# Attention scores of units 10 to 35 from float16 halves that transfers make

## The chip, the cores and the metric

One core of a Trainium2 chip runs the whole program in one launch. The metric is the device time of one execution in microseconds, the median of several runs. The engines are TensorE (PE; its weight loads are shown as PEld), VectorE (DVE), ScalarE (ACT), GpSimd (POOL) and SyncE (SP), and 16 DMA engines move data.

## The reference, cut to what matters

Attention within chunks of 64 positions, then two feed-forward stages, of which only the first lines bear on the change:

```python
scores = scale * np.matmul(q_c, k_c.transpose(0, 1, 2, 4, 3))     # 64x64 per chunk and head
scores = scores - np.max(scores, axis=-1, keepdims=True)
attn = np.exp(scores)
attn = attn / (np.sum(attn, axis=-1, keepdims=True) + 1e-09)
out = np.matmul(attn, v_c)
...
xn = (x - mu) / np.sqrt(var + 1e-06) * g_ln
ch = np.maximum(xn @ w_ch1, 0.0) @ w_ch2
return (x + ch).astype(np.float32)
```

There are 8 batches, 8 heads and 576 positions (9 chunks of 64), model width 512 and a feed-forward width of 2048. A third stage (`_moe2_ref`) follows and is not touched.

## The kernel before

**Units and blocks.** The 72 chunks of all batches are taken two at a time: 36 units, numbered 0 to 35, of 128 rows x 512. Two units make a block; 18 blocks go through the first feed-forward stage. `attention(t)` (L301) does one unit, `norm` (L439) its layer norm, and a DMA transpose (`transpose`, L265) puts the normalised rows, as two float16 halves, into the tile `xT` of the block. The products of the first feed-forward layer (`ff1p`, L737, its matmul at L750) read `xT`; those of the second (`ff2p`, L786, matmul at L802) read its results from `arena`. From block 3 on, one step of a block is 24 matmuls of L750 and 21 of L802, and a block has eight steps.

**Halves.** A float32 operand is split into a float16 `hi` and the float16 remainder `lo`, and a product is done as hi*hi + hi*lo + lo*hi, three float16 matmuls.

**A unit.** `scores(t)` (L279) loads q and k of the unit by one transfer on SP (L283) into a float32 tile, `qk` or, from unit 10 (`JOIN`) on, the single buffer `qkl`, and does 16 float32 matmuls of 64x64 (L291). VectorE takes maxima (L389) and subtracts them (L390), ScalarE takes the exponentials (L393). Up to unit 13 (`BYDMA` is 14) the probabilities are turned by four float32 matmuls against the identity (L337), copied from PSUM by ScalarE (`pt`, L416), and multiplied with v by 16 float32 matmuls (L361). From unit 14 on, ScalarE and VectorE split them into halves (`ph`, L400 and L401), a DMA transpose on SP turns these (`ptt`, L404), v is split as well (`vq`, L408 and L409), and 48 float16 matmuls of 64x64 do the product (L349). VectorE then divides (L430), takes the statistics (L462, L463), POOL the inverse root (L457, L460), VectorE normalises (L466), ScalarE and POOL make the two halves `hl` (L469, L471), and SP issues the transpose into `xT` (L474).

**Joint steps.** From unit 10 on the values product of a unit and the scores of the next are one item of TensorE's queue (L429):

```python
scores(t + 1, o)
a_, qk_ = started[t + 1]
o("PE", 1260, lambda: (pv_(), qk_()), rd=pp() + [a_], wr=[kp, ks])
```

**What sets the order.** Everything is recorded first (`Plan.op`) with an engine, an assumed duration, a priority and an assumed delay to its users on other engines (`lat`). `Plan.run` then deals the items out greedily, each engine taking the item of lowest priority number among those that its model holds ready, and so fixes the order of each engine's queue. Each engine runs its queue strictly in that order. A unit t has priority 10t and goes ahead of the feed-forward products, at 1000 and above, as soon as the model holds its inputs ready.

Of the kernel before, what the change touches and what calls it, by code (L numbers as in the profile page):

```python
# [9 lines left out]
F16 = mybir.dt.float16  # L10
F32 = mybir.dt.float32
# [3 lines left out]
AF = mybir.ActivationFunctionType  # L15
ALU = mybir.AluOpType
# [8 lines left out]
    a=[2264, -1991, -1698, -26, -1734, 4025, 2562, -374],  # L25
# [15 lines left out]
    f=[-277, -1680, 2543],  # L41
# [106 lines left out]
def fused_kernel(ctx: ExitStack, tc, qkv, w1, w2, g1, w_in, w_out, wsgt, wsgs, g2, b_sg, out):  # L148
# [122 lines left out]
    def palloc(tag, bufs, shape, dt, pool=None):  # L271
        return plan.buf(tag, bufs, lambda: (pool or pools["att"][1]).tile(shape, dt, tag=tag, name=tag, bufs=bufs))
# [1 line left out]
    x_t = {}  # L274
    xT_t = {}
    started = {}
    BYDMA = 14

    def scores(t, o):  # L279

        a = palloc("qk", 2, [P, 2, 512], F32) if t < JOIN else palloc("qkl", 1, [P, 2, 512], F32)
        src = qkv[t].rearrange("p (a f) -> p a f", a=3)
        o("SP", 1700, lambda: nc.sync.dma_start(out=a.t, in_=src[:, 0:2]), wr=[a], lat=2200 if t < JOIN else 4000)  # L283
        s2 = pair[t % 2 if t < 6 else 1]

        def qk():
            for hp in range(4):
                for r in (slice(0, 64), slice(64, 128)):
                    for c in range(2):
                        k = hp * 128 + c * 64  # L290
                        nc.tensor.matmul(  # L291
                            s2[64 * c:64 * c + 64, r.start // 64, hp * 64:hp * 64 + 64],
                            lhsT=a.t[r, 0, k:k + 64],
                            rhs=a.t[r, 1, k:k + 64],
                            start=True,
                            stop=True,
                        )

        started[t] = a, qk

    def attention(t):  # L301
        n = t % 2 if t < 6 else 1
# [7 lines left out]
        def o(eng, ns, fn, **k):  # L310
            ns = FAST.get((eng, ns), ns)
            op(eng, ns, fn, prio=k.pop("prio", pr), lat=k.pop("lat", lat), **k)

        if t not in started:
            scores(t, o)
            a, qk = started[t]
            o("PE", 1260 * z, qk, rd=[a], wr=[ks])
        v = palloc("v", 2, [P, 512], F32) if t < JOIN else palloc("vl", 1, [P, 512], F32)
        o("SP", 730, lambda: nc.sync.dma_start(out=v.t, in_=qkv[t].rearrange("p (a f) -> p a f", a=3)[:, 2]), wr=[v], lat=2200)
        mx = palloc("mx", 2, [P, 2, 4, 1], F32)  # L320
        pm = palloc("pm", 2, [P, 4, 2, 64], F32) if t < JOIN else palloc("pml", 1, [P, 4, 2, 64], F32)
        sm = palloc("sm", 2, [P, 4, 2, 1], F32)
        rd = palloc("rd", 2, [P, 4, 2, 1], F32)
        pt = palloc("pt", 1, [P, 4, 128], F32) if t < BYDMA else None
        if t in (4, 5):
            x = plan.buf(f"x{t}", 1, lambda: pools["att"][1].tile([P, 512], F32, name=f"x{t}", bufs=1))
        else:
# [13 lines left out]
        def pv_():  # L341
            if t >= BYDMA:
                for hp in range(4):
                    for n, (y, z) in enumerate(((0, 0), (0, 1), (1, 0))):
                        for r in (slice(0, 64), slice(64, 128)):
                            for c in range(2):
                                k = c * 256 + hp * 64
                                q = hp * 128 + c * 64
                                nc.tensor.matmul(  # L349
                                    s2[64 * c:64 * c + 64, r.start // 64, 256 + hp * 64:256 + hp * 64 + 64],  # L350
                                    lhsT=ptt[0].t[r, y, q:q + 64],
                                    rhs=vq[0].t[r, z, k:k + 64],
                                    start=(n == 0),
                                    stop=(n == 2),
                                )
                return
            for hp in range(4):
                for r in (slice(0, 64), slice(64, 128)):
                    for c in range(2):
                        k = c * 256 + hp * 64  # L360
                        nc.tensor.matmul(  # L361
                            s2[64 * c:64 * c + 64, r.start // 64, 256 + hp * 64:256 + hp * 64 + 64],
                            lhsT=pt.t[r, hp, 64 * c:64 * c + 64],
                            rhs=v.t[r, k:k + 64],
                            start=True,
                            stop=True,
                        )
# [56 lines left out]
        if t < JOIN or t + 1 == NT:  # L424
            o("PE", 1260 * z, pv_, rd=pp(), wr=[kp])
        else:
            scores(t + 1, o)
            a_, qk_ = started[t + 1]
            o("PE", 1260, lambda: (pv_(), qk_()), rd=pp() + [a_], wr=[kp, ks])  # L429
        o("DVE", 600, lambda: nc.vector.tensor_tensor(  # L430
            out=x.t.rearrange("p (h a d) -> p a h d", h=4, a=2),
            in0=pv,
# [6 lines left out]
    def norm(t, x, o):  # L439

        bs = palloc("bs", 2, [P, 6], F32)
        mv = palloc("mv", 2, [P, 2], F32)
        rs = palloc("rs", 2, [P, 1], F32)
        xn = palloc("xn", 1, [P, 512], F32)
        hl = palloc("hl", 2, [P, 2, 512], F16)
        b = t // 2
        c0 = (t % 2 if b < B0 else 1 - t % 2) * 128
        if t % 2 == 0:
            if b == 2:
                xT_t[b] = plan.buf("xT2", 1, lambda: stage.tile([P, 2, 4, 256], F16, name="xT2"))  # L450
            else:
                xT_t[b] = palloc("xT", 2, [P, 2, 4, 256], F16, px)
        xT = xT_t[b]
        x_t[t] = x

        def rs_():
            nc.gpsimd.tensor_scalar(  # L457
                out=rs.t, in0=mv.t[:, 1:2], scalar1=1.0, scalar2=1e-6, op0=ALU.mult, op1=ALU.add
            )
            nc.gpsimd.tensor_tensor(out=rs.t, in0=rs.t, in1=cpow, op=ALU.pow)  # L460

        o("DVE", 600, lambda: nc.vector.bn_stats(out=bs.t, in_=x.t), rd=[x], wr=[bs])  # L462
        o("DVE", 70, lambda: nc.vector.bn_aggr(out=mv.t, in_=bs.t), rd=[bs], wr=[mv])  # L463
        o("POOL", 730, rs_, rd=[mv, "cpow"], wr=[rs], two=2)
        xe = ("POOL", 830, nc.gpsimd) if t < 8 and TUNE['xn'][t] else ("DVE", 460, nc.vector)
        o(xe[0], xe[1], lambda: xe[2].tensor_scalar(  # L466
            out=xn.t, in0=x.t, scalar1=mv.t[:, 0:1], scalar2=rs.t, op0=ALU.subtract, op1=ALU.mult
        ), rd=[x, mv, rs], wr=[xn], two=1 + (xe[0] == "POOL"))
        o("ACT", 520, lambda: nc.scalar.activation(out=hl.t[:, 0], in_=xn.t, func=AF.Copy), rd=[xn], wr=[hl])  # L469
        lo = ("DVE", 600, nc.vector) if t < 8 and TUNE['lo'][t] else ("POOL", 1110, nc.gpsimd)  # L470
        o(lo[0], lo[1], lambda: lo[2].tensor_tensor(  # L471
            out=hl.t[:, 1], in0=xn.t, in1=hl.t[:, 0], op=ALU.subtract
        ), rd=[xn], wr=[hl], two=1)
        o("SP", 1100, lambda: transpose(xT.t, slice(c0, c0 + 128), hl.t), rd=[hl], wr=[xT], lat=2200)  # L474
# [379 lines left out]

    bW = {"top": Buf("topB", None)}

    ATT = [f"{n}{k}" for n in ("qk", "v", "mx", "pm", "sm", "rd", "bs", "mv", "rs", "hl") for k in range(2)] + ["pt", "xn", "qkl", "vl", "u0", "u1", "pml", "ph", "ptt", "vq"]
    w2s = {}

    def open_sums():  # L860
# [822 lines left out]
```

## Time and profile before

| | |
|---|---|
| median of 3 runs | 1177.54 us (1176.41 to 1178.52) |
| the profiled execution | 1177.76 us, of which the span of its trace is 1175.7 us |
| TensorE matmul busy | 1163.7 us, 99% of the span |
| VectorE busy | 915.2 us, 78% |
| ScalarE busy | 586.3 us, 50% |
| GpSimd busy | 196.5 us, 17% |

A share of busy time is an average over stages. Block 3 begins at 178.7 us of the span, units 10 to 35 lie between there and 697 us, and the third stage follows from about 800 us on. Times of instructions are taken by the hardware profiler; matmuls overlap each other, so that the time which a group of them adds to TensorE's queue is read from the starts of its neighbours, and not from the duration of one.

### The profile page before, as it was taken

The page shows a single profiled execution, that of the slowest core. Times are in us where ns is not written, and L with a number is a line of the kernel's source. Part 1 is how long each engine was busy: PE and PEld are TensorE (multiplying, and loading weights), DVE is VectorE, ACT ScalarE, POOL GpSimd, SP SyncE. Part 2 cuts the span into 40 slices and gives each one's busy share as a digit, 9 for nine tenths or more (in the row PEclk, how much of TensorE's full clock was granted, in tenths as well). Part 3 has the DMA queues.
Part 4 walks back from the last instruction along what each step waited for, and adds up shares of the span by engine and source line. Part 5 has one row for each costly group of instructions (what it writes and reads, how often), then busy time and mean ns, then how long its engine had stood idle before and what let it go on. Part 6 is the DMA issues. An engine that isn't in the chain of part 4 may idle for free.

```text
span 1175.7 us, 27945 instructions
## 1 busy us (share of the span) xinstructions
PE 1163.7 (99%) x11810; PEld 884.4 (75%) x11810; DVE 915.2 (78%) x1744; ACT 586.3 (50%) x854; POOL 196.5 (17%) x279
## 2 busy tenths in 40 slices
PE   8899999999999999999999999999999999999998
PEld 6687448888888888888888888888565566557454
DVE  6997797898898888768877865677889589577555
ACT  5787634665665644434444443345646445434330
POOL 2211010323113112211311322012102001102100
PEclk7999999999999999999999999999999999999999
DMA  8974016544242343244133111436175573372303
GB/s 286 281 242 118 18 28 225 185 111 91 75 93 69 68 100 91 65 82 91 55 89 75 56 46 33 88 86 179 38 140 158 113 149 110 91 123 73 90 1 117
DMA packets 165053, 124.36 MB, mean 106 GB/s; under 512 B 128704, under 2 KB 137792, under 8 KB 164928
## 3 DMA queue, kind: packets, MB, share of 16 engines
q1 hardware_dynamic: 164928, 122.58, 40.2%
q8 instruction: 92, 1.51, 0.5%
q14 instruction: 33, 0.27, 0.1%
HBM read 72.74 MB, written 18.88 MB: 78 GB/s over the span
## 4 chain that ended last, share of the span: by engine, by line
PE 92%; DVE 4%; DMA 2%; ACT 1%; issue 1%; POOL 0%; SPq 0%; ACTq 0%; DVEq 0%
PE bank L750 26%; PE acc L802 23%; PE pb L1478 5%; PE acc L1562 4%; PE pair L659 4%; PE pb L1562 4%; PE acc L1478 3%; PE pb L1382 3%; PE bank L638 3%; PE acc L1424 3%; PE pb L1424 3%; PE acc L1382 3%; PE bank L659 2%; PE pair L291 1%; PE pair L349 1%; PE pb L1479 1%
## 5 line engine op out<-in xcount | busy, mean ns | idle before, releaser
L750 PE MATMUL bank<-xT,w1h 128*128 128x256 f16 x1920 | 321.0, 273 | 0.0
L802 PEld LDWEIGHTS <-arena 128*128 128x128 f16 x2520 | 244.5, 98 | 29.7 <-DVE arena L778 0.2
L750 PE MATMUL bank<-xT,w1l 128*128 128x256 f16 x960 | 261.7, 273 | 0.0
L802 PE MATMUL acc<-w,arena 128*128 128x256 f16 x1440 | 218.3, 273 | 0.0
L750 PEld LDWEIGHTS <-w1h 128*128 128x128 f16 x1920 | 187.7, 98 | 22.1
L777 ACT ACTIVATE arena<-arena 128x896 f16<-128x896 f32 x120 | 113.9, 949 | 159.3 <-DVE arena L774 75.4
L802 PE MATMUL acc<-w2s,arena 128*128 128x256 f16 x1080 | 177.2, 273 | 0.0
L778 DVE TENSOR_TENSOR arena<-arena 128x896 f16<-128x896 f32 x120 | 130.3, 1086 | 39.5 <-ACT arena L777 39.1
L765 ACT ACTIVATE arena<-bank 128x512 f32<-128x512 f32 x120 | 71.4, 595 | 121.2 <-PE bank L750 120.6
L835 POOL TENSOR_TENSOR x<-x,u 128x256 f32<-128x256 f32 (+1 forms) x65 | 62.6, 989 | 259.2 <-DVE x L825 157.7
L750 PEld LDWEIGHTS <-w1l 128*128 128x128 f16 x960 | 93.9, 98 | 10.8
L772 DVE TENSOR_TENSOR arena<-arena 128x256 f32<-128x256 f32 x120 | 57.2, 477 | 37.1 <-ACT arena L765 36.1
L1562 PEld LDWEIGHTS <-w2s 128*128 128x128 f16 x444 | 43.4, 98 | 47.3
L1382 PEld LDWEIGHTS <-x2T 128*128 128x128 f16 x672 | 65.6, 98 | 9.8
L638 PE MATMUL bank<-xT,w1h 128*128 128x256 f16 x384 | 64.4, 273 | 1.1 <-DMA xT<-hl 0.7
L773 DVE TENSOR_TENSOR arena<-arena 128x256 f32<-128x256 f32 x120 | 59.1, 492 | 4.1
L1424 PEld LDWEIGHTS <-late 128*128 128x128 f16 x336 | 32.7, 98 | 39.2
L471 POOL TENSOR_TENSOR hl<-xn,hl 128x512 f16<-128x512 f32 x32 | 43.1, 1346 | 72.9 <-ACT hl L469 68.6
L1478 PEld LDWEIGHTS <-vh 128*128 128x128 f16 x288 | 28.6, 99 | 33.2
L1562 PE MATMUL acc<-wout,w2s 128*128 128x512 f16 (+1 forms) x252 | 53.3, 369 | 0.0
L638 PE MATMUL bank<-xT,w1l 128*128 128x256 f16 x192 | 52.3, 273 | 0.0
L1478 PE MATMUL pb<-wsg,vh 128*128 128x512 f16 x166 | 51.6, 380 | 0.0
(287 smaller groups left out, 2050.7 us busy)
## 6 DMA issues: line engine op xcount, KB each, us to landing
straw<-in_w SPq DMA_DIRECT2D x16, 1023.8 KB, 6.2
qkl<-in_qkv SPq DMA_DIRECT2D x26, 512.0 KB, 3.9
x2d<-x SPq DMA_DIRECT2D x36, 256.0 KB, 2.0
xs<-x2d SPq DMA_DIRECT2D x27, 256.0 KB, 4.2
vl<-in_qkv SPq DMA_DIRECT2D x26, 256.0 KB, 3.2
w2s<-x2d SPq DMA_DIRECT2D x21, 256.0 KB, 2.8
out<-w2s SPq DMA_DIRECT2D x21, 256.0 KB, 3.1
qk<-in_qkv SPq DMA_DIRECT2D x10, 512.0 KB, 4.8
```

Source lines behind the costliest of these rows:

```text
L638: nc.tensor.matmul(acc, lhsT=w[j][:, k, fc], rhs=xT.t[:, x, k], start=(n == 0), stop=(n == 11))
L659: nc.tensor.matmul(acc[i], lhsT=h[x].t[:, c], rhs=w2t[j][:, f % 2, y], start=(f == 0 and n == 0), stop=(f == NF - 1 and n == 2),)
L750: nc.tensor.matmul(acc[:, y * 256:y * 256 + 256], lhsT=w[j][:, k, fc], rhs=xT.t[:, x, k], start=(n == 0), stop=(n == 11),)
L765: op("ACT", 500, lambda: nc.scalar.activation(out=o.t[:, 0:4].rearrange("p n t -> p (n t)"), in_=acc, func=AF.Relu, scale=0.5), rd=[kb] + ...
L777: op("ACT", 860, lambda: nc.scalar.activation(out=h.t[:, 0], in_=o.t[:, 1:8], func=AF.Copy), rd=[o] + ar, wr=[h], prio=-100)
L778: op("DVE", 1010, lambda: nc.vector.tensor_tensor(out=h.t[:, 1], in0=o.t[:, 1:8], in1=h.t[:, 0], op=ALU.subtract), rd=[o, h], wr=[h.key + ...
L802: nc.tensor.matmul(acc, lhsT=h.t[:, x, n], rhs=r(y), start=(first and j == 0 and m == 0), stop=(j == 7 and m == 2), skip_group_check=True,)
L835: op("POOL", ns, lambda: nc.gpsimd.tensor_tensor(out=d(), in0=d(), in1=v(), op=ALU.add), rd=u + ["q6", "q5", "q7"], wr=[x], prio=-50, two=1)
L1382: nc.tensor.matmul(ap[:, q * 256:q * 256 + 256], lhsT=xT[:, x, a, k, c], rhs=right(b, 1, k, w), start=(first and n == 0), stop=(k == 1 and ...
L1424: nc.tensor.matmul(ap, lhsT=right(b, 0, k, w)[:, m * 128:m * 128 + 128], rhs=xT[:, x, a, k], start=(first and n == 0), stop=(k == 1 and w ...
L1478: nc.tensor.matmul(ap, lhsT=v[:, fc], rhs=w[:, 0:512], start=(n == 0), stop=end)
L1562: nc.tensor.matmul(ap[:, 0:m], lhsT=x[:, k, c], rhs=w[:, k, fc], start=(n == 0), stop=(n == 11))
```

## The change

For units 10 to 35, the float32 load of q and k on SP is replaced by three steps. POOL's queue issues a transfer that converts q and k to float16 on the way into `qh`; ScalarE writes its negative into `ql`; POOL's queue issues a second transfer from the same float32 source that adds into `ql`, which leaves the low half there. `qh` and `ql` have two buffers each, in place of the single float32 `qkl`. The scores are then 48 float16 matmuls in place of 16 float32 ones.

`BYDMA` goes from 14 to 10: units 10 to 13 also take the way of the halves, with the DMA transpose and the float16 values product, and the four transposes by matmul (L337) and the copy (L416) of these units go. For units from 10 on, the tile of the normalised halves (`hl`, two buffers) becomes `hll` with one. The assumed delays of units 10 to 13 follow `BYDMA`.

```diff
-    BYDMA = 14
+    BYDMA = 10
...
     def scores(t, o):
 
-        a = palloc("qk", 2, [P, 2, 512], F32) if t < JOIN else palloc("qkl", 1, [P, 2, 512], F32)
         src = qkv[t].rearrange("p (a f) -> p a f", a=3)
-        o("SP", 1700, lambda: nc.sync.dma_start(out=a.t, in_=src[:, 0:2]), wr=[a], lat=2200 if t < JOIN else 4000)
         s2 = pair[t % 2 if t < 6 else 1]
+        if t >= JOIN:
+            hi, lo = (palloc(n, 2, [P, 2, 512], F16) for n in ("qh", "ql"))
+            o("POOL", 700, lambda: nc.gpsimd.dma_start(out=hi.t, in_=src[:, 0:2]), wr=[hi], lat=7000)
+            o("ACT", 1050, lambda: nc.scalar.activation(out=lo.t, in_=hi.t, func=AF.Copy, scale=-1.0), rd=[hi], wr=[lo], lat=3000)
+            o("POOL", 920, lambda: nc.gpsimd.dma_start(
+                out=lo.t, in_=src[:, 0:2], accum_op=ALU.add
+            ), wr=[lo], lat=8000)
+
+            def qk():
+                for hp in range(4):
+                    for n, (y, z) in enumerate(((hi, hi), (hi, lo), (lo, hi))):
+                        for r in (slice(0, 64), slice(64, 128)):
+                            for c in range(2):
+                                k = hp * 128 + c * 64
+                                nc.tensor.matmul(
+                                    s2[64 * c:64 * c + 64, r.start // 64, hp * 64:hp * 64 + 64],
+                                    lhsT=y.t[r, 0, k:k + 64],
+                                    rhs=z.t[r, 1, k:k + 64],
+                                    start=(n == 0),
+                                    stop=(n == 2),
+                                )
+
+            started[t] = [hi, lo], qk
+            return
+        a = palloc("qk", 2, [P, 2, 512], F32)
+        o("SP", 1700, lambda: nc.sync.dma_start(out=a.t, in_=src[:, 0:2]), wr=[a], lat=2200)
...
-        hl = palloc("hl", 2, [P, 2, 512], F16)
+        hl = palloc("hl", 2, [P, 2, 512], F16) if t < JOIN else palloc("hll", 1, [P, 2, 512], F16)
```

The scheduler makes a new order of all queues from this. Three places of it matter here. The names of the tiles are those of the code; line numbers of the changed kernel are 30 higher below the edit.

The first is the fetch of units 10 and 11 (q and k, v), at the start of block 3. Before, it stands in SP's queue:

```order
L283 DMA qkl<-in_qkv 128x1024
L319 DMA vl<-in_qkv 128x512
L479 DMA raw<-in_w_in 128x4095
L906 DMA wsg<-in_wsgt 128x576 x3
L283 DMA qkl<-in_qkv 128x1024
```

After, it is POOL's queue that issues it, for units 10 to 13 in this order (`rs` and `x` behind it are the norm of unit 10 and the residual of block 3):

```order
L285 DMA qh_2401<-in_qkv 128x1024
L285 DMA qh_2417<-in_qkv 128x1024
L287 DMA ql_2526<-in_qkv 128x1024
L287 DMA ql_2544<-in_qkv 128x1024
L285 DMA qh_2745<-in_qkv 128x1024
L287 DMA ql_2877<-in_qkv 128x1024
L285 DMA qh_3027<-in_qkv 128x1024
L487 TENSOR_SCALAR rs_3077<-mv_3067 128x1
L490 TENSOR_TENSOR rs_3077<-rs_3077,cpow_129 128x1
L865 TENSOR_TENSOR x_1396<-x_1396,u_3064 128x512
```

What moved: the loads of q and k left SP, and each unit now has two issues on POOL, in one queue with the norm and the residual.

The second is ScalarE's queue where the copies `ql` of units 10 and 11 stand, among the steps of the feed-forward stage (`arena` from a bank is the step that empties a PSUM bank):

```order
L795 ACTIVATE arena_123<-bank2_68 128x512
L516 ACTIVATE top_2428<-raw_2431 128x1024
L807 ACTIVATE arena_123<-arena_123 128x896
L286 ACTIVATE ql_2526<-qh_2401 128x1024
L795 ACTIVATE arena_123<-bank3_69 128x512
L286 ACTIVATE ql_2544<-qh_2417 128x1024
```

What moved: the copy, which waits for the first transfer, stands ahead of the emptying of a bank.

The third is SP's queue where block 5's `xT` is written. Before:

```order
L283 DMA qkl_2839<-in_qkv 128x1024
L267 DMA_TRANSPOSE xT_2886<-hl_2767 128x8x128
L479 DMA raw_2906<-in_w_in 128x4095
L267 DMA_TRANSPOSE xT_2886<-hl_2936 128x8x128
L479 DMA raw_3041<-in_w_out 128x4095
```

After:

```order
L434 DMA_TRANSPOSE ptt_2840<-ph_2811 128x8x128
L509 DMA raw_2885<-in_w_out 128x4095
L981 DMA redd0_72<-redc_140 128x1
L343 DMA vl_3103<-in_qkv 128x512
L707 DMA x2d6_81<-x_1396 128x512
L707 DMA x2d7_82<-x_1558 128x512
L434 DMA_TRANSPOSE ptt_3251<-ph_3100 128x8x128
L267 DMA_TRANSPOSE xT_3289<-hll_3246 128x8x128
```

What moved: the transposes of probabilities of units 10 and 11 now stand in this queue, ahead of the transpose into `xT`.

On TensorE the score steps of the first units come later among the feed-forward products, and the later units catch up. Counted over TensorE's order, in products of L750 and L802 since the start of block 3:

| step | before | after |
|---|---|---|
| scores of unit 10 | 84 | 240 |
| values of 10, scores of 11 | 168 | 360 |
| values of 11, scores of 12 | 252 | 567 |
| values of 12, scores of 13 | 375 | 699 |
| first product with `xT` of block 5 | 678 | 705 |
| values of 13, scores of 14 | 567 | 807 |
| values of 14, scores of 15 | 690 | 972 |
| values of 25, scores of 26, and all later ones | 2652 | 2652 |

## Rows read from the trace of the kernel before

**Rows 1.** The page, part 1: busy time, share of the span, instructions of each engine.

```profile
PE 1163.7 (99%) x11810; PEld 884.4 (75%) x11810; DVE 915.2 (78%) x1744; ACT 586.3 (50%) x854; POOL 196.5 (17%) x279
```

**Rows 2.** The page, part 4: the chain that ended last, shares by engine.

```profile
PE 92%; DVE 4%; DMA 2%; ACT 1%; issue 1%; POOL 0%; SPq 0%; ACTq 0%; DVEq 0%
```

**Rows 3.** Windows: busy us (instructions) of PE, PEld, DVE, ACT, POOL; clock, DMA share, GB/s.

```profile
180.00:220.00 40.00, 40.00 (x500) 35.56 (x498) 33.12 (x64) 23.64 (x33) 6.03 (x6) 1.00 0.70 221
220.00:260.00 40.00, 40.00 (x475) 35.62 (x474) 37.17 (x78) 25.46 (x40) 11.53 (x12) 1.00 0.44 143
260.00:300.00 40.00, 40.00 (x578) 35.44 (x576) 35.08 (x73) 23.45 (x36) 10.03 (x11) 1.00 0.47 95
460.00:500.00 40.00, 40.00 (x508) 35.58 (x507) 30.77 (x60) 17.30 (x26) 8.38 (x11) 1.00 0.33 75
```

**Rows 4.** Waits of TensorE's matmuls: line, released by, us in total, times, longest.

```profile
PE pair L349 <- DMA ptt<-ph: 0.6, 1, 0.6
```

**Rows 5.** Timeline of TensorE at unit 10's scores: start us, us, engine line op.

```profile
187.42 0.49 PE L802 MATMUL acc<-w2s,arena 128*128 128x256 f16 x3
...
188.47 0.72 PE L802 MATMUL acc<-w,arena 128*128 128x256 f16 x5
```

**Rows 6.** The same timeline at unit 10's values and unit 11's scores.

```profile
197.76 0.49 PE L802 MATMUL acc<-w2s,arena 128*128 128x256 f16 x3
198.18 0.69 PE L361 MATMUL pair<-vl,pt 64*64 64x64 f32 x32
...
199.27 0.39 PE L802 MATMUL acc<-w,arena 128*128 128x256 f16 x2
```

**Rows 7.** The same timeline at a joint step with float16 values, float32 scores.

```profile
336.77 0.49 PE L802 MATMUL acc<-w2s,arena 128*128 128x256 f16 x3
337.19 0.58 PE L349 MATMUL pair<-vq,ptt 64*64 64x64 f16 x48
337.59 0.69 PE L291 MATMUL pair<-qkl 64*64 64x64 f32 x32
338.22 0.50 PE L802 MATMUL acc<-w,arena 128*128 128x256 f16 x3
```

**Rows 8.** The same timeline at unit 10's transposes by matmul.

```profile
194.05 0.60 PE L337 MATMUL pair<-ident,pml 128*128 128x128 f32 x4
194.48 0.49 PE L802 MATMUL acc<-w2s,arena 128*128 128x256 f16 x3
```

**Rows 9.** DMA issues by line: count, KB, median us from issue to landing.

```profile
qkl<-in_qkv SPq DMA_DIRECT2D x26, 512.0 KB, 3.9
xT<-hl SPq DMA_TRANSPOSE x36, 3.4
redd<-redc SPq DMA_DIRECT2D x3, 0.5 KB, 9.7
```

**Rows 10.** Timeline: SP's first load of unit 10; unit 11's values product and transpose.

```profile
180.72 0.33 SPq L283 DMA_DIRECT2D qkl<-in_qkv  x1
...
208.98 0.69 PE L361 MATMUL pair<-vl,pt 64*64 64x64 f32 x32
...
220.88 1.24 SPq L267 DMA_TRANSPOSE xT<-hl  x1
```

**Rows 11.** Groups by line, VectorE and ScalarE: xcount, busy us, mean ns, idle before.

```profile
L401 DVE TENSOR_TENSOR ph<-pml,ph 128x512 f16<-128x512 f32 x22 | 15.9, 724 | 0.0
L912 ACT ACTIVATE tmp<-late 128x1024 bf16<-128x1024 f32 x4 | 4.2, 1057 | 0.8 <-DVE late L491 0.7
```

**Rows 12.** Timeline of GpSimd around unit 11's norm.

```profile
214.78 1.07 POOL L457 TENSOR_SCALAR rs<-mv 128x1 f32<-128x1 f32 x1 [5.27 <-DVE mv L463]
```

**Rows 13.** Timeline of SP's queue and ScalarE after a late joint step.

```profile
448.22 0.33 SPq L283 DMA_DIRECT2D qkl<-in_qkv  x1
451.59 0.60 ACT L765 ACTIVATE arena<-bank 128x512 f32<-128x512 f32 x1 [1.73 <-PE bank L750]
456.51 0.60 ACT L765 ACTIVATE arena<-bank 128x512 f32<-128x512 f32 x1
```

More of the change, by code (lines that the diff above doesn't have):

```diff
@@ L297, in qk @@
                         )
-        started[t] = a, qk
+        started[t] = [a], qk
     def attention(t):
@@ L316, in attention @@
             a, qk = started[t]
-            o("PE", 1260 * z, qk, rd=[a], wr=[ks])
+            o("PE", 1260 * z, qk, rd=a, wr=[ks])
         v = palloc("v", 2, [P, 512], F32) if t < JOIN else palloc("vl", 1, [P, 512], F32)
@@ L323, in attention @@
         rd = palloc("rd", 2, [P, 4, 2, 1], F32)
-        pt = palloc("pt", 1, [P, 4, 128], F32) if t < BYDMA else None
+        pt = None
+        if t < JOIN:
+            pt = palloc("pt", 1, [P, 4, 128], F32)
+        elif t < BYDMA:
+            pt = plan.buf("ptt", 1, lambda: pools["att"][1].tile(
+                [P, 2, 512], F16, tag="ptt", name="ptt", bufs=1
+            ).rearrange("p x f -> p (x f)").bitcast(F32).rearrange("p (h q) -> p h q", h=4))
         if t in (4, 5):
@@ L428, in attention @@
             a_, qk_ = started[t + 1]
-            o("PE", 1260, lambda: (pv_(), qk_()), rd=pp() + [a_], wr=[kp, ks])
+            o("PE", 1260, lambda: (pv_(), qk_()), rd=pp() + a_, wr=[kp, ks])
         o("DVE", 600, lambda: nc.vector.tensor_tensor(
@@ L855, in fused_kernel @@
     bW = {"top": Buf("topB", None)}
-    ATT = [f"{n}{k}" for n in ("qk", "v", "mx", "pm", "sm", "rd", "bs", "mv", "rs", "hl") for k in range(2)] + ["pt", "xn", "qkl", "vl", "u0", "u1", "pml", "ph", "ptt", "vq"]
+    ATT = [f"{n}{k}" for n in ("qk", "v", "mx", "pm", "sm", "rd", "bs", "mv", "rs", "hl") for k in range(2)] + ["pt", "xn", "qh0", "qh1", "ql0", "ql1", "hll", "vl", "u0", "u1", "pml", "ph", "ptt", "vq"]
     w2s = {}
```

## Prediction

> **What bounds the kernel now.** I read the page's busy shares first, then its chain, then the waits, and then timelines. TensorE is busy for 1163.7 of 1175.7 us [rows 1] and makes up 92% of the chain that ended last [rows 2], so what counts is how long its queue is. The windows show the stage of the change, 180 to 700 us: TensorE busy for 40.00 of 40 us, granted clock 1.00, that is 2.4 GHz, while VectorE has 2.8 to 9.2 us idle and ScalarE 14.5 to 22.7 [rows 3]. In the whole span the values products of the units wait for the transposed probabilities once, for 0.6 us [rows 4]. So each instruction taken off TensorE in this stage shortens the run, as long as the new producers of its operands are in time. The sum is made against the profiled execution, 1177.76 us, of which its span is 1175.7; the median of the runs is 0.22 us lower.
>
> **What TensorE loses.** Feed-forward matmuls start 0.109 us apart, three in 0.33 us, so what a step adds is the start of its successor less the start of the three before it, less 0.33.
>
> - Scores alone, unit 10: 188.47 - 187.42 - 0.33 = 0.72 us [rows 5].
> - Joint step with both products in float32, units 10 to 13: 199.27 - 197.76 - 0.33 = 1.18 us [rows 6].
> - Joint step with values in float16 halves, units 14 to 34, 21 of them: 338.22 - 336.77 - 0.33 = 1.12 us. In it the 48 float16 matmuls take 337.59 - 337.19 = 0.40 us, the float32 scores 338.22 - 337.59 = 0.63, and 0.09 is lost on entry [rows 7].
> - Transposes by matmul, units 10 to 13: 194.48 - 194.05 = 0.43 us each, without a gap on entry [rows 8].
>
> The new scores are 48 float16 matmuls of 64x64 in the same pattern of tiles as the values product, so I take the same 0.40 us: 0.49 alone, 0.89 in a joint step. The bounds are 0.40 and the 0.63 of float32. Unit 10 then saves 0.23, four joint steps 0.29 each, 21 joint steps 0.23 each, and four groups of transposes 0.43 each: 0.23 + 1.16 + 4.83 + 1.72 = **7.94 us**. The values product of unit 35 stands alone and stays.
>
> The Trainium skill (FP8 and Floating Point Precision, TensorE Precision Notes) says that a true float32 product takes four passes through the array. By that rule three float16 products would cost three quarters of 0.63, or 0.47 us, as an estimate, and the 26 scores would save 4.2 us in place of 6.0; the trace gives 0.40 for the same pattern of float16 matmuls, and the measurement decides.
>
> **What the new producers cost.** Each unit now needs two transfers issued by POOL with ScalarE's copy between them.
>
> - The transfers. No trace shows a transfer from POOL's queue, a converting or an adding one. The nearest row is the load of the same 512 KB by SP, 3.9 us; the slowest in the list is 9.7 us, for a store with little data [rows 9]. An issue on POOL I put between its shortest instructions, nothing next to the rest, and 1.24 us, what SP's queue spends on a transpose [rows 10]. ScalarE's copy is 1.06 us, from the row of 128x1024 [rows 11]. The chain is then 9 us at the low end (3.9 + 1.06 + 3.9) and 23 at the high one (1.24 + 9.7 + 1.06 + 1.24 + 9.7). I take 11, the low end with both issues, since that row moves the same bytes.
> - The room for it. From unit 12 on, the first transfer can go when the scores two units before have freed the buffer. In the order that is at least 240 feed-forward products earlier (unit 14: 567 to 807), 240 x 0.109 + two joint steps = 28 us. For unit 10 the fetch can go at 181 us, as the load did [rows 10], and its scores stand 156 products later than their 187.8 us, at 205 us: 24 us. Both hold the 23 us, so I cost the chain at nothing. If it runs longer, TensorE waits for all of the excess.
> - ScalarE: 26 copies, 27 us over 510, less four copies from PSUM, plus eight halves for units 10 to 13. It is hidden by the 22.7 us of 40 that ScalarE stands idle [rows 3]. Behind the copy in ScalarE's queue stands the emptying of a PSUM bank, which TensorE waits for if the copy waits; see the second rival.
> - VectorE: eight more halves (`ph` and `vq` of units 10 to 13) at 0.72 us [rows 11], 5.8 us in 180 to 300 us, where it has 120 - 105.4 = 14.6 us idle [rows 3]. Hidden, but the cover becomes thin, at 2.8 us in 220 to 260.
> - SP loses 26 loads and gains four transposes. The DMA engines carry the same source once more per unit: at 3.9 us of everything, two units in 40 us add at most 0.2 to a share of 0.33 [rows 3, 9]. Nothing for the bandwidth, but a transpose can land later.
> - One buffer `hll`: the halves of a unit wait until the transpose of the one before has landed, 3.4 us [rows 9]. In the late stage `xT` is needed a block later, so it is free.
>
> **What is late next.** Before, units 10 and 11 were done long before block 5 needed them. In the new order the first product of block 5 stands 138 products and a joint step behind the values product of unit 11, 138 x 0.109 + 0.9 + 0.9 = 16.8 us. The trace of before needs, for the same unit, 220.88 - 208.98 + 3.4 = 15.3 us from that product to a landed `xT` [rows 9, 10], and one more half on VectorE makes it 16.0. That fits with less than 1 us to spare. Units 10 and 11 can each be late by a little, and a transpose of probabilities that meets the new transfers can hold a values product. Bounds for all new waits of TensorE: -0.6 us (the one wait in the trace goes too) and 8 us (the first rival). I take **2 us**, nearer the low end, since the order leaves room at all the other steps.
>
> Sum: 1177.76 - 7.94 + 2.0 = 1171.8 us against the profiled execution, 1171.6 against the median.
>
> **Rivals.**
>
> 1. *VectorE becomes the bound in 180 to 340 us, and nothing is gained.* POOL and VectorE hold each other up: POOL's `rs` on 128x1 takes 1.07 us when VectorE is busy [rows 12]. If an issue on POOL holds VectorE for 0.9 us, the 17 issues that the order brings up to 300 us (both of units 10 to 17, the first of unit 18) cost 15.3 us; with the halves 21.1, 6.5 more than the 14.6 idle. TensorE's feed lags by that and by idle time that can't be used, 8 us in all, in place of the 2 us above: 1171.6 - 2 + 8 = 1177.6 us. For it speaks the busy share of 37.17 in 40; against it, that the preparation of later weights, which fills VectorE there, can slide behind 300 us. Chance 0.13. The Trainium skill (SBUF — State Buffer, SBUF: two separate sides) says that GpSimd can't write its descriptors while VectorE runs an operation that takes both ports; by that rule the transfers would start late rather than VectorE, and no run here shows how late.
> 2. *ScalarE waits for the first transfer, and the kernel gets slower.* ScalarE's copy of a unit stands behind the second relu after the joint step: in before's times at 457.1 us, 9 us after the joint step at 448.2 [rows 13]. A transfer that lands later holds ScalarE, with the emptying of the bank behind it; ScalarE has 1.73 us idle per step there [rows 13]. So a first transfer of up to about 10 us costs nothing, and beyond that each excess us reaches TensorE in each of 26 units. At 0.3 us too much the gain is gone; at 0.5, 26 x 0.5 = 13 us, the time is 1177.5 - 7.9 + 13 = 1182.6 us. For it: nothing shows the speed of a converting transfer. Against it: 512 KB land in 3.9 us from SP. Chance 0.12.
> 3. *The halves save less on TensorE.* Three products accumulate into one place, and if they run at the float32 step's 0.63 us, only the transposes and the values of units 10 to 13 are won: 1.72 + 0.44 = 2.2, and with 2 us of waits the time is 1177.4 us. At half way between 0.40 and 0.63 it is 1174.6. Against it: the values product accumulates in the same way [rows 7]. Chance 0.07. By the rule of four passes above, with 0.47 us, it would be 1173.4.
>
> **How the numbers follow.** The forecast has a chance of 0.68. About 0.2%, or 2.4 us, is what a measurement of this kernel can tell from no change: faster ends at 1175.2, slower begins at 1179.9. Faster: 0.68 and half of rival 3, less 0.02 for a forecast whose waits grow to 6 us, 0.70. Same: rival 1, the other half of rival 3 and those waits, 0.18. Slower: rival 2, 0.12. The range goes from 1168.0 (with no waits it is 1169.6, less the 0.6, and another 1.0 if the new step takes 0.36 us) to 1178.0, which takes in rivals 1 and 3; what is left out is rival 2 and a few hundredths.
>
> **What would show it.** Right: the joint step takes 0.89 us in the timeline and the groups of TensorE's transposes at units 10 to 13 are gone; its busy time falls by about 8 us; the waits list for TensorE stays within a few us, the longest near 200 to 260 us, on `xT` or the turned probabilities. Wrong: waits of TensorE on `ql` (the chain is longer than its room), ScalarE idle before the copies with TensorE idle on a bank (rival 2), VectorE at 40 of 40 us in the windows to 300 us (rival 1), or a scores step above 0.45 us (rival 3).

## The result and the profile after

The changed kernel is slower: 1188.56 us (median of 6 runs, 1186.75 to 1192.67) against 1178.17 us (6 runs) of the kernel before, a ratio of 1.0095 with a 95% interval of 1.0081 to 1.0108. The forecast was 1171.6 us, faster. The profiled execution took 1187.24 us, its span 1185.5.

The page of the changed kernel: busy times; POOL's queue among the DMA queues (packets, MB, share of the 16 engines' span); the chain that ended last; issues with their median us to landing.

```profile
PE 1160.3 (98%) x12274; PEld 878.4 (74%) x12274; DVE 915.5 (77%) x1752; ACT 609.6 (51%) x884; POOL 234.8 (20%) x331
...
q0 software_dynamic: 7488, 13.63, 10.0%
...
PE 76%; DMA 10%; DVE 8%; ACT 3%; issue 2%; POOL 1%; SPq 0%; ACTq 0%; DVEq 0%; POOLq 0%
...
qh<-in_qkv POOLq DMA_DIRECT2D x26, 256.0 KB, 4.2
ql<-in_qkv POOLq DMA_DIRECT2D x26, 256.0 KB, 6.0
```

TensorE's busy time fell by 3.4 us only [rows 1], its idle time grew by 13.2 (1185.5 - 1160.3 against 1175.7 - 1163.7), and the chain now runs through DMAs for 10% of the span, where it was 2% [rows 2]. VectorE is as busy as before. The windows show where:

```profile
180.00:220.00 40.00, 39.78 (x407) 35.22 (x405) 29.19 (x55) 24.73 (x33) 3.65 (x5) 1.00 0.76 213
220.00:260.00 40.00, 38.08 (x517) 33.27 (x518) 37.54 (x74) 24.67 (x38) 14.22 (x16) 1.00 0.65 126
260.00:300.00 40.00, 35.78 (x587) 31.34 (x585) 30.57 (x64) 24.49 (x39) 12.73 (x17) 1.00 0.90 95
460.00:500.00 40.00, 40.00 (x541) 35.60 (x540) 32.17 (x63) 18.92 (x27) 13.16 (x17) 1.00 0.50 85
```

From 220 to 300 us TensorE has 6.1 us idle, where it had none [rows 3]. The DMA engines are busy for 0.90 of 260 to 300 us, before 0.47, and move no more: 95 GB/s then and now. And TensorE's waits from 178 to 720 us:

```profile
PE pair L379 <- DMA ptt<-ph: 5.3, 8, 2.0
PE acc L832 <- DVE arena L808: 1.3, 3, 0.7
PE bank L780 <- DMA xT<-hll: 1.2, 1, 1.2
PE acc L832 <- DVE u L855: 1.0, 2, 0.7
PE acc L832 <- ACT arena L807: 0.8, 1, 0.8
```

The turned probabilities were waited for once before, for 0.6 us [rows 4]; now eight times, for 5.3. `ql` is not in the list: no scores step waited.

**Where 9.8 us come from** (the two spans, worked out from the starts of TensorE's matmuls in both traces). Block 3 begins 1.1 us later, though TensorE's order up to there is the same: a difference between executions. From its first product to the last of L832, 621.9 us became 630.0. In that stretch the attention steps cost 4.4 us less, and idle time grew by 12.5 us: 5.8 in eight joint steps less the 0.7 of before, and 7.4 between feed-forward products. The third stage takes 371.9 us in both, and the last 0.6 us lie behind it.

**What a joint step costs now**, in TensorE's timeline of the changed kernel (the step follows three products that start at 362.97):

```profile
362.97 0.49 PE L832 MATMUL acc<-w,arena 128*128 128x256 f16 x3
363.39 0.58 PE L379 MATMUL pair<-vq,ptt 64*64 64x64 f16 x48
363.79 0.21 PE L297 MATMUL pair<-qh 64*64 64x64 f16 x4
...
364.18 0.22 PE L297 MATMUL pair<-qh,ql 64*64 64x64 f16 x4
364.33 0.50 PE L832 MATMUL acc<-w,arena 128*128 128x256 f16 x3
```

364.33 - 362.97 - 0.33 = 1.03 us, not 0.89. The 12 groups of scores start 0.03 to 0.05 us apart, 0.39 us from first to last, but the next product starts 0.15 after the last group, some 0.12 more than a group takes. The way from a float16 step back to the feed-forward products costs this, and the trace of before had such a step: unit 35's values alone, a row that the prediction did not use.

```profile
696.04 0.49 PE L802 MATMUL acc<-w,arena 128*128 128x256 f16 x3
696.47 0.57 PE L349 MATMUL pair<-vq,ptt 64*64 64x64 f16 x48
696.97 0.50 PE L802 MATMUL acc<-w,arena 128*128 128x256 f16 x3
```

696.97 - 696.04 - 0.33 = 0.60 us. The 0.40 that I used is the distance to a float32 step [rows 7]. Unit 10's scores now take 0.60 too.

**How a transpose gets late.** The same values step, unit 26, in both traces. Before: the transpose's issue on SP, the values on TensorE.

```profile
499.19 1.24 SPq L404 DMA_TRANSPOSE ptt<-ph  x1
...
504.19 0.58 PE L349 MATMUL pair<-vq,ptt 64*64 64x64 f16 x48
```

After: the same two, and POOL's second transfer for unit 28 between them.

```profile
506.38 1.24 SPq L434 DMA_TRANSPOSE ptt<-ph  x1
...
506.62 0.91 POOL L287 DMA_DIRECT2D ql<-in_qkv  x1 [2.62 <-ACT ql L286]
...
511.76 0.58 PE L379 MATMUL pair<-vq,ptt 64*64 64x64 f16 x48 [0.34 <-DMA ptt<-ph]
```

The joint steps before these stand at 488.44 and 495.69, so the transpose is issued at the same distance, 10.7 us. It landed 3.1 us after its issue then, with 1.9 us to spare, and 5.3 us after it now. TensorE's order is the same in both kernels here. ScalarE's copy of `qh` sets the time of POOL's issue, and it stands where the halves of the probabilities are made, so the two transfers meet in every second late unit.

### The profile page after: what moved, and what is told of

Same layout as the page of the kernel before. It is cut to its first block, busy times and chain, and to the rows that moved or that the text cites. A ratio compares the mean times of both kernels' runs of the same rounds, so it can differ in the third digit from the quotient of the medians.

```text
span 1185.5 us, 28990 instructions
## 1 busy us (share of the span) xinstructions
PE 1160.3 (98%) x12274; PEld 878.4 (74%) x12274; DVE 915.5 (77%) x1752; ACT 609.6 (51%) x884; POOL 234.8 (20%) x331
## 3 DMA queue, kind: packets, MB, share of 16 engines
q0 software_dynamic: 7488, 13.63, 10.0%
## 4 chain that ended last, share of the span: by engine, by line
PE 76%; DMA 10%; DVE 8%; ACT 3%; issue 2%; POOL 1%; SPq 0%; ACTq 0%; DVEq 0%; POOLq 0%
PE bank L780 18%; PE acc L832 15%; PE pb L1508 5%; PE acc L1592 4%; PE bank L668 4%; PE pair L689 4%; PE pb L1592 3%; PE acc L1508 3%; PE pb L1412 3%; PE acc L1454 3%; PE pb L1454 3%; DMA ptt<-ph 3%; PE acc L1412 3%; PE bank L689 2%; DMA xT<-hll 1%
## 5 line engine op out<-in xcount | busy, mean ns | idle before, releaser
L832 PEld LDWEIGHTS <-arena 128*128 128x128 f16 x2520 | 244.1, 98 | 35.0 <-DVE arena L808 2.4
L780 PE MATMUL bank<-xT,w1l 128*128 128x256 f16 x960 | 261.8, 273 | 0.0
L832 PE MATMUL acc<-w,arena 128*128 128x256 f16 x1440 | 218.7, 273 | 3.8 <-ACT arena L807 1.5
L832 PE MATMUL acc<-w2s,arena 128*128 128x256 f16 x1080 | 177.2, 273 | 0.0
L802 DVE TENSOR_TENSOR arena<-arena 128x256 f32<-128x256 f32 x120 | 59.6, 497 | 39.2 <-ACT arena L795 38.9
L865 POOL TENSOR_TENSOR x<-x,u 128x256 f32<-128x256 f32 (+1 forms) x65 | 59.1, 933 | 71.2 <-ACT arena L807 35.1
L501 POOL TENSOR_TENSOR hll<-xn,hll 128x512 f16<-128x512 f32 x26 | 36.7, 1410 | 125.6 <-ACT hll L499 125.6
L1359 POOL TENSOR_SCALAR rs<-mv 128x2 f32<-128x2 f32 (+1 forms) x20 | 6.4, 319 | 260.4 <-DVE mv L1354 258.4
L487 POOL TENSOR_SCALAR rs<-mv 128x1 f32<-128x1 f32 x36 | 12.3, 343 | 207.2 <-DVE mv L493 205.1
```

What stands on the lines that cost most here:

```text
L780: nc.tensor.matmul(acc[:, y * 256:y * 256 + 256], lhsT=w[j][:, k, fc], rhs=xT.t[:, x, k], start=(n == 0), stop=(n == 11),)
L802: nc.vector.tensor_tensor(out=two(6, 8), in0=two(1, 3), in1=two(0, 2), op=ALU.subtract)
L832: nc.tensor.matmul(acc, lhsT=h.t[:, x, n], rhs=r(y), start=(first and j == 0 and m == 0), stop=(j == 7 and m == 2), skip_group_check=True,)
```

## The experiments

Theory A: POOL's transfers hold the DMA engines and slow what runs beside them, the transposes above all. Theory B: the waits come from the longer way of units 10 to 13 and the new order, whatever carries q and k. Theory C: VectorE and ScalarE have no room. Each edit makes the scheduler order the queues anew, except where the text says that an order is kept. Medians, and ratios to the kernel before on the same chip:

| run | kernel | us | ratio (95%) |
|---|---|---|---|
| e1 | before, `BYDMA` 10 | 1175.28 | 0.9974 (0.9964 to 0.9983) |
| e2 | change, `BYDMA` 14 | 1184.85 | 1.0055 (1.0040 to 1.0071) |
| e3 | change, halves without POOL | 1176.08 | 0.9982 (0.9967 to 0.9996) |
| e4 | e5 and POOL's two transfers, unused | 1199.96 | 1.0189 (1.0172 to 1.0206) |
| e5 | e1, one buffer `hll` | 1176.12 | 0.9986 (0.9976 to 0.9995) |
| e6 | e5 and two loads on SP, unused | 1180.03 | 1.0017 (1.0006 to 1.0029) |
| e7, e12 | change, second transfer later | 1193.33, 1192.45 | 1.0119 (1.0101 to 1.0137), e12 |
| e8 | e1, halves without POOL from unit 20 | 1173.60 | 0.9968 (0.9955 to 0.9981) |
| e9 | e4, no conversion | 1187.66 | 1.0080 (1.0059 to 1.0101) |
| e10, e11 | e8 from unit 16, from 14 | 1175.11, 1173.57 | 0.9973 (0.9959 to 0.9986), 0.9968 (0.9956 to 0.9980) |

**e1, the transposes alone.** The only edit is `BYDMA = 10` in the kernel before.

> The kernel before with BYDMA = 10 and nothing else: units 10 to 13 take the way of the halves, the scores stay float32 from one load on SP, no transfer on POOL. TensorE saves four groups of transposes at 0.44 us and 4 x 0.07 us in the joint steps, 2.0 us. Theory A (the waits of the changed kernel come from POOL's transfers, which hold the DMA engines and slow the transposes): 1176 us, 1175 to 1177, and waits for turned probabilities of under 1 us. Theory B (the waits of 220 to 300 us come from the longer way of units 10 to 13 and the order it makes, POOL's transfers or not): the 6 us of idle TensorE in 220 to 300 us stay, 1178.2 - 2 + 5 = 1181 us.

Faster, and TensorE waits for turned probabilities once, for 0.5 us. This half of the change pays, by about 3 us. So the longer way alone does not bring the waits. The new order is not covered by this: unit 10's scores stand behind 84 products in e1, as before, and behind 240 in the change, and no run has the changed kernel's order without POOL's transfers. For the stage in which TensorE's order differs, that part of theory B stays untried.

**e2, the scores alone.** The changed kernel with `BYDMA = 14`.

> The changed kernel with BYDMA = 14 again: float16 scores from POOL's transfers, but units 10 to 13 turn their probabilities by matmul. TensorE saves 0.12 us at unit 10 and about 0.09 us in each of 25 joint steps, 2.4 us. Theory A: the waits on turned probabilities of the late units (0.4 to 0.5 us, four of them) and some of the early ones stay, 5 to 10 us in all: 1181 to 1186 us. Theory B: without the longer way of units 10 to 13 the waits are gone: 1175 to 1177 us.

1184.85: as A has it. TensorE waits seven times for turned probabilities, 4.8 us. The two halves do not add up: -3 and +6.5 us apart, +11 together. Only together do the transposes of units 10 to 13 run in the stage where POOL's transfers are slowest, which may be why; it was not tried.

**e3, the same scores without POOL.**

```diff
-            hi, lo = (palloc(n, 2, [P, 2, 512], F16) for n in ("qh", "ql"))
-            o("POOL", 700, lambda: nc.gpsimd.dma_start(out=hi.t, in_=src[:, 0:2]), wr=[hi], lat=7000)
-            o("ACT", 1050, lambda: nc.scalar.activation(out=lo.t, in_=hi.t, func=AF.Copy, scale=-1.0), rd=[hi], wr=[lo], lat=3000)
-            o("POOL", 920, lambda: nc.gpsimd.dma_start(
-                out=lo.t, in_=src[:, 0:2], accum_op=ALU.add
-            ), wr=[lo], lat=8000)
+            f = palloc("qkl", 1, [P, 2, 512], F32)
+            hi, lo = (palloc(n, 1, [P, 2, 512], F16) for n in ("qh", "ql"))
+            o("SP", 1700, lambda: nc.sync.dma_start(out=f.t, in_=src[:, 0:2]), wr=[f], lat=4000)
+            o("ACT", 1050, lambda: nc.scalar.activation(out=hi.t, in_=f.t, func=AF.Copy), rd=[f], wr=[hi])
+            o("DVE", 1150, lambda: nc.vector.tensor_tensor(out=lo.t, in0=f.t, in1=hi.t, op=ALU.subtract), rd=[f, hi], wr=[lo], two=1)
```

> The changed kernel with the same float16 scores and BYDMA = 10, but q and k come by one float32 load on SP, and ScalarE copies the high half and VectorE subtracts to the low one (one buffer each). TensorE's work is that of the changed kernel, 4.4 us under the kernel before; VectorE gets 26 x 1.1 = 29 us more. Theory A: the waits on turned probabilities go to under 1 us, and 1174 to 1177 us result, unless VectorE's new work makes waits of its own. Theory C (VectorE and ScalarE have no room, the transfers are harmless): as slow as the changed kernel or slower, 1187 us and more, with the waits in 180 to 340 us larger than before.

TensorE does the work of the changed kernel, VectorE more, and the time is 12 to 13 us shorter, so that the whole loss is gone. 1176.08 us is in A's range; the waits for turned probabilities, 1.1 us, are just above A's 1 us. TensorE's waits from 178 to 720 us:

```profile
PE bank L779 <- issue: 3.6, 1, 3.6
PE pair L378 <- DMA ptt<-ph: 1.1, 1, 1.1
```

Theory C falls as the main cause: VectorE has 455.2 us of 520 to do between 180 and 700 us (before 429.0), and TensorE waits for it nowhere in this list. The 3.6 us are a pause at 310 us for which the profile shows no wait.

**e5 and e4, the transfers alone.** e5 is e1 with `hll` as in the change. e4 adds to it, for units from 10 on:

```diff
+            hi, lo = (palloc(n, 1, [P, 2, 512], F16) for n in ("qh", "ql"))
+            o("POOL", 700, lambda: nc.gpsimd.dma_start(out=hi.t, in_=src[:, 0:2]), rd=[a], wr=[hi], lat=7000)
+            o("POOL", 920, lambda: nc.gpsimd.dma_start(out=lo.t, in_=src[:, 0:2]), rd=[hi], wr=[lo], lat=8000)
```

> The kernel of e1 with one buffer of normalised halves in place of two, as the changed kernel has it: the exact base of e4. Theory A: the single buffer costs nothing that can be measured, 1175 to 1177 us, and nearly all of what e4 lost is the transfers'. If the single buffer is a second cause (ScalarE waited 2.8 us for it at 438 us in the changed kernel), 1178 to 1182 us, with ScalarE and then TensorE late behind the waiting half.

> The kernel of e1 with one buffer of normalised halves, and both of POOL's converting transfers of each unit from 10 on issued into tiles that nobody reads: scores stay float32, ScalarE's copy is left out. TensorE's work is that of e1. Theory A: the transfers alone bring waits on turned probabilities and on xT, 5 to 10 us: 1181 to 1186 us, with the transposes at 5 us and more to landing where a transfer runs beside them. Theory B or C: as e1 within 2 us.

One buffer costs nothing here that can be told (1176.12 against 1175.28, intervals overlap). Transfers that nobody reads cost 1.0189 - 0.9986 of 1178 us = 24 us, far above the 5 to 10 that A expected. In e4 both go at once, while ScalarE's copy lies between them in the change; and e4 keeps SP's load of q and k, which the change takes away. What each of the two makes was not tried. (e4's second transfer does not add, and its profiled execution, 1193.57 us, is the fastest of its five, so that its trace shows less than the whole loss.) TensorE waits eight times for turned probabilities, 8.1 us, and once for 7.1 us on VectorE, which waited for a store (below).

**e6 and e9, what about these transfers.** e9 is e4 with the order of every queue kept, but float32 tiles of 128x512 as targets, so nothing is converted; e6 issues the same two loads on SP.

> The kernel of e5 and two transfers more per unit, as in e4 and into tiles of the same size that nobody reads, but issued by SP and float32 on both sides: 128 rows of 2 KB each, as many bytes written as in e4. Theory A1 (POOL's queue is the cost: its 2 KB packets take 0.17 to 0.25 us in the changed kernel, those of SP 0.08): 1175 to 1178 us, as e5. Theory A2 (any transfer more in this stage crowds the transposes): as e4, 1185 us and more.

> The kernel of e4 with the order of every queue as there and the same number of transfers on POOL, but float32 on both sides, 128 rows of 2 KB each: as many bytes written, no conversion. If POOL's queue itself is the cost, about 1200 us as e4. If the conversion is, about 1180 us as e6, with packets of 2 KB at 0.08 us in place of 0.17 to 0.25.

No expectation of the two held. Against e5, two more loads on SP cost 3.7 us, on POOL's queue 11, and converting 24. Converting goes with twice the bytes read, 4 KB of float32 for each 2 KB written, and the two were not tried apart. The share of the DMA engines differs, for the same 13.63 MB written. e4, POOL's queue and the median landing of `ptt`:

```profile
q0 software_dynamic: 7488, 13.63, 8.0%
...
ptt<-ph SPq DMA_TRANSPOSE x26, 5.1
```

e9, the same:

```profile
q0 software_dynamic: 4160, 13.63, 4.4%
...
ptt<-ph SPq DMA_TRANSPOSE x26, 3.5
```

And SP's queue, first e5, then e6:

```profile
q1 hardware_dynamic: 169152, 123.63, 40.9%
```

```profile
q1 hardware_dynamic: 176640, 137.27, 43.9%
```

On SP the 13.63 MB add 3.0 points, on POOL's queue 4.4, converted 8.0, and 10.0 in the changed kernel. The step from 4.4 to 8.0 fits the bytes read: by the packets of these traces from 455 to 700 us (medians), a converting packet that reads 4 KB takes 0.17 us in e4, a plain packet of 4 KB takes 0.16 on POOL's queue in e9 and 0.16 on SP's queue in the kernel before. An adding packet takes 0.25 in the changed kernel.

Call what lies behind product 2652 the calm stage, and what lies between there and the start of block 3 the crowded one. In the calm stage, where the order of TensorE is that of before, e9 and e6 take as long as before (312.1 us from there to the last feed-forward product of the stage), e4 takes 316.0 and the changed kernel 314.0, though its attention steps are shorter. So there only the transfers that convert, with their doubled reading, cost TensorE anything.

What remains of e9 is one pause of TensorE in the crowded stage, 10.1 us. It stands behind VectorE, which waits for a store of `x2d` that SP issued 2.2 us ahead of POOL's two transfers (rows of SP, POOL and VectorE).

```profile
273.23 0.32 SPq L681 DMA_DIRECT2D x2d<-x  x1
273.60 0.42 SPq L955 DMA_DIRECT2D redd<-redc  x1
...
275.45 0.56 POOL L286 DMA_DIRECT2D qh<-in_qkv  x1
276.01 0.55 POOL L287 DMA_DIRECT2D ql<-in_qkv  x1
...
290.37 0.69 DVE L434 TENSOR_TENSOR x<-pair,rd 128x512 f32<-128x512 f32 x1 [12.86 <-DMA x2d<-x]
```

Such a store lands after 2.0 us in the median; the longest took 17.1 us in e9, 15.8 in e4, 14.1 in e12, 10.8 in e6, 10.0 in the changed kernel, 5.3 before and 4.5 in e3. But it took 10.7 us in e1, 10.4 in e5, 10.5 in e8 and 11.1 in e11 too, without any transfer on POOL's queue, and VectorE did not wait for it there. So this stretch is slow without POOL's transfers as well. In these traces every store that took 10 us and more was issued within 8 us of `redd<-redc`, a store of 0.5 KB on SP, which took 17.0 us itself in the rows above; whether that store is the cause was not tried. Nor do the runs show how much of e9's pause is POOL's queue, and how much is that its order puts an instruction of VectorE close behind the late store.

**e7 and e12, the collision moved.** In the changed kernel, `lat=9000 if t > 26 else 3000` in place of `lat=3000` at ScalarE's copy; TensorE's order stays as it is, and every second late `ql` goes behind the next joint step. e7 is a single execution, e12 the same kernel with a median of 6.

> The changed kernel, except that from unit 27 on the second transfer (the adding one) of every second unit is issued some 6 us later, behind the next joint step, and so not beside the transpose of the probabilities of units 26 to 32; TensorE's order is the same. Theory A: the transposes of those units land in 3.1 us again, in place of 5.3, and the four waits of 0.39 to 0.50 us at about 512 to 637 us are gone, 1.8 us. If the waits have another cause (a later half on VectorE, say), they stay.

> The kernel of e7 once more, timed, since its one execution held a stall of 6.9 us at 276 us that its rows put down to no wait, in a stage where its order is that of the changed kernel. Theory A: the trace again shows transposes of 3.0 to 3.1 us for units 26 to 32 and joint steps of 1.03 us there; the time is the changed kernel's 1.0095 of before less 1.8 us, or 1.008, unless such stalls, which come and go between executions, cover it: then 1.008 to 1.012. If the stall comes in every execution, 1.013 and a trace that shows it again.

The mechanism holds. The `ptt` of units 26, 28, 30 and 32 land after 3.0 to 3.1 us in both, and the joint steps that took 1.44, 1.52, 1.53 and 1.42 us take 1.03. The meeting is moved rather than gone: in e12 the transposes of units 27, 29 and 31 land after 6.0, 7.5 and 4.3 us (3.2, 4.8 and 3.3 in the changed kernel), but these have the room and hold nothing. The time does not follow. In e12 three other joint steps of that stage wait, 1.7 us together, for VectorE's division of an earlier unit, such as

```profile
543.81 0.57 PE L379 MATMUL pair<-vq,ptt 64*64 64x64 f16 x48 [0.64 <-DVE x L460]
```

The moved issue now stands between POOL's residual additions, and VectorE stood 2.4 us behind these ahead of that division. But in the changed kernel it stands 2.4 us behind them at the same place (at 532 us), without the issue between, so the moved issue is not shown to be the cause; it stays open. From product 2652 on, e12 takes 313.9 us, e7 312.8, the changed kernel 314.0. The larger part is in the crowded stage, where their order is that of the changed kernel: its 316.0 us from block 3 to product 2652 became 324.1 and 322.6, mostly by single pauses at 276 us of 6.9 us (e7, no wait shown)

```profile
282.91 0.37 PE L832 MATMUL acc<-w2s,arena 128*128 128x256 f16 x1 [6.92 <-issue]
```

and of 4.9 us (e12, for `ptt`), where the changed kernel's profiled execution had 0.95. So the pauses of that stage vary between these three executions, and the changed kernel's, at 1187.24 us, is the third fastest of its six. That e12 is slower in every execution for another reason is not ruled out: its median is 1192.45 us against 1188.56, with intervals that overlap.

**e8, e10 and e11, towards a better kernel.** e1, with e3's halves from unit 20, 16 or 14 on and float32 scores for the units before.

> A version that could beat both: the kernel of e1, no transfer on POOL, float32 scores up to unit 19, and from unit 20 on the scores in float16 halves that ScalarE and VectorE make of the float32 load, as in e3. TensorE saves 16 x 0.09 = 1.4 us against e1. Theory A: 1173 to 1175 us, as VectorE has 5 us and more idle in each 40 us there. Theory C (no room on VectorE): 1176 us and more, with waits on turned probabilities behind 380 us.

> The kernel of e8 with float16 halves from unit 16 on in place of 20: 4 x 0.09 = 0.4 us less on TensorE, 4 x 1.2 us more on VectorE in 320 to 390 us. Theory A: 1173 to 1174 us. If VectorE's room ends there, 1175 us and more.

> The same from unit 14 on: 0.2 us less on TensorE than e10, and VectorE's additional work reaches into 280 to 320 us. Theory A: 1173 to 1174 us. If VectorE has no room there, 1175 us and more, near e3's 1176.

All beat both kernels, by 0.3% against the kernel before; they cannot be told from each other or from e1 by time. e8 and e11 came out as A has it, e10 at 1175.11 us where A had 1173 to 1174. By the trace, block 3 to the last product takes 621.0 us in e1, 618.8 in e8, 618.4 in e10 and 617.9 in e11, so the float16 scores come out 2 to 3 us ahead where nothing is put on POOL's queue. Of that the steps themselves make 1.4 to 2.0, at 0.09 us each; the rest is that e1 pauses a little more. e8's only wait in the list of TensorE from 178 to 830 us:

```profile
PE pair L379 <- DMA ptt<-ph: 0.6, 1, 0.6
```

## Why the prediction was wrong

- **What TensorE loses: 7.94 us forecast, 4.4 found.** Unit 10's scores saved 0.12 (0.23 forecast), four joint steps 0.16 each (0.29), 21 joint steps 0.09 each (0.23), four transposes 0.44 each (0.43). The term "the same 0.40 us" failed: it was read from a step that a float32 step follows, and a float16 step ahead of feed-forward products costs 0.60. The rival that the halves save less was half right; its mechanism, accumulation at the float32 pace, was not (0.03 us per group of four, as for the values). Its 0.44 us for the values of units 10 to 13 was also too much: the joint steps differ by 0.06 us each (1.18 and 1.12), 0.24 in all. The 26 scores saved 2.4 us by the trace, where the forecast had 6.0. The Trainium skill (FP8 and Floating Point Precision, TensorE Precision Notes) has true float32 as four passes through the array, from which the prediction estimated 4.2 us. That estimate was nearer than 6.0, but the 2.4 measured here is still well under it.
- **The chain of the new producers, costed at nothing: right.** 4.2 us for the first transfer, 1.04 for the copy, 6.0 for the second, issues of 0.58 and 0.90 at the start of the two transfers, 11.2 us in all by these medians (11 forecast), in room of 24 us and more; no scores step waited. The upper bound of 23 us was too low: unit 15's chain took 25.4 us, from an issue at 263.1 us to the second landing at 288.5, and its scores stand at 298.
- **All new waits of TensorE, 2 us, at most 8: this step failed, with 12.5 us, and it turned the sign.** The place was named ("a transpose of probabilities that meets the new transfers can hold a values product"; "a transpose can land later"), but the DMA engines were costed by bytes, from SP's 3.9 us for the same load. In the late stage that sum was right: a share of at most 0.2 more on 0.33, and 0.50 came. In 260 to 300 us it went from 0.47 to 0.90 without more bytes. e3 (the same scores without the transfers) and e4 against e5 (the transfers without the scores) show that the transfers are the cause; the order of the queues changes with them in both. In the calm stage, where TensorE's order stays, the transpose of unit 26 beside a transfer of POOL (5.3 us to landing, 3.1 without) shows how. In the crowded stage, where most of the 12.5 us lie, how much is the transfers and how much the order was not tried apart, nor what POOL's queue has to do with it. The Trainium skill (DMA: Bandwidth & Descriptors, Issuing engines are not separate DMA queues) says that transfers from all engines run on the same 16 DMA engines and interleave. The 5.3 us agree with it.
- **What is late next: right place.** The first product of block 5 waited for `xT`, 1.4 us at 263 us, where less than 1 us had been left.
- **Rival 1, VectorE the bound: no.** VectorE was busy for 915.5 us, as before, and for 30.6 of 40 us in the window where TensorE lost most; POOL's issues did not lengthen it.
- **Rival 2, ScalarE waits for the first transfer: seen, for up to 3.9 of the 12.5 us.** ScalarE waited for it four times, 7.5 us in all, in the crowded stage. The first transfer of unit 13 took 13.3 us. ScalarE stood 3.47 us behind it, and two feed-forward steps lost 1.85 us together (ScalarE's row, then TensorE's):

```profile
234.75 1.06 ACT L286 ACTIVATE ql<-qh 128x1024 f16<-128x1024 f16 x1 [3.47 <-DMA qh<-in_qkv]
...
236.70 0.39 PE L832 MATMUL acc<-w,arena 128*128 128x256 f16 x2 [0.79 <-ACT arena L807]
```

 The first transfer of unit 16 took 11.4 us and held ScalarE for 2.41. Behind the copy in ScalarE's queue stand the halves of unit 14's probabilities, so their transpose went out late, and it landed late, after 5.9 us (rows of ScalarE, SP and TensorE):

```profile
289.80 1.06 ACT L286 ACTIVATE ql<-qh 128x1024 f16<-128x1024 f16 x1 [2.41 <-DMA qh<-in_qkv]
290.76 0.61 ACT L430 ACTIVATE ph<-pml 128x512 f16<-128x512 f32 x1
...
292.17 2.26 SPq L434 DMA_TRANSPOSE ptt<-ph  x1
...
298.09 0.58 PE L379 MATMUL pair<-vq,ptt 64*64 64x64 f16 x48 [2.03 <-DMA ptt<-ph]
```

 That is the longest of TensorE's waits; by these rows, the late issue or the late landing alone would have been covered. From unit 25 on these transfers land within 3.6 to 4.3 us and ScalarE is not held. So rival 2, which had "slower" at a chance of 0.12, holds for a part of the loss, and not in each of the 26 units; the larger part came by a mechanism that the forecast had priced at 2 us.

Not settled: what share of the 11 us of POOL's queue is the queue itself and what the moment at which its transfers go out, and what the pauses without a shown wait are (0.4 us at 319 us in the changed kernel, 1.6 in e2, 3.6 in e3, 6.9 in e7).

## What to carry to other kernels

Cost a new transfer not only by its own landing but by what lands later beside it: list the transfers that TensorE waits for soonest, with their slack, and take a few us from each that a converting transfer can meet. Where an engine has idle time, a copy and a subtraction there can be cheaper than a conversion on the way, as e3 shows against the change. And read a step's price from a place with the same neighbours on both sides, since the time to leave it shows only before some successors.

## What was not expected of the hardware

- The time for which a converting transfer holds the DMA engines goes with what it reads rather than with what it writes: 13.63 MB written took 8.0% of their time on POOL's queue in e4, 4.4% there without conversion, and a converting packet that reads 4 KB takes about as long as a plain one of 4 KB (0.17 against 0.16 us). One that adds takes 0.25 us, and the share is 10.0% in the changed kernel.
- A transpose that lands in 3.1 us alone took 5.3 us beside one adding transfer, though SP issued the one and POOL the other.
- A store of 256 KB that lands after 2.0 us in the median took 10 to 11 us once or twice in kernels without a transfer on POOL's queue (e1, e5, e8, e11), in a stretch that also holds a store of 0.5 KB.
- A float16 64x64 step costs some 0.12 us on the way out to 128x128 products, and nothing between two such steps (0.60 us alone, 1.03 for two).
- A pause costs more than itself: after the one of 3.65 us in e3, products started 0.21 us apart for about 25 products, the lower of the two levels of TensorE's clock, 1.2 GHz; over 300 to 340 us the granted clock is 0.91, and 1.00 in the 40 us before.

```profile
300.00:340.00 40.00, 36.35 (x483) 31.09 (x481) 29.39 (x59) 22.15 (x30) 9.66 (x10) 0.91 0.49 60
```
